# Loading the two halves of the query weights' rows from two queues in a decode attention kernel

## The chip, the cores and the metric

One core of one Trainium2 chip. The time is the device time of one execution in microseconds (us); lower is better. The kernel before takes 196.1 us (median of 5 runs, 195.98 to 196.16). In the profiles PE is the tensor engine, DVE the vector engine, ACT the scalar engine, POOL GpSimd and SP the sync engine.

## The reference

Four tokens go through a gated mix of an attention block with a sliding window and a ReGLU block. Cut to what matters:

```python
# x: [4, 1, 512], 32 query heads, 8 K/V heads, head size 128, window W = 4096
q = (x @ wq)                       # wq: [512, 4096] bf16, 4 MB: the load that the change splits
k = k_cache[:, :, Sk - W:, :]      # 4 x 8 x 4096 x 128, 32 MB
v = v_cache[:, :, Sk - W:, :]      # 32 MB
a = softmax(q k^T / sqrt(128)) v @ wo      # wo: 4 MB
b = (relu(x @ W_gate) * (x @ W_up)) @ W_down   # 3 x 1.75 MB
g = sigmoid((x * gate_w).sum(-1))
out = g * a + (1 - g) * b
```

Each input byte is used once. The sizes above, in units of 2^20 bytes, add up to 77.25, so at least 81 million bytes (81 MB) have to be moved for every execution.

## The kernel before

Everything large comes in through four SBUF slots of 128 partitions x 32 KB. All loads are issued by the sync engine, in one fixed order, on one queue (the list in which transfers wait for the DMA engines; the prediction also says ring). A load waits until the slot that it takes is free. The first four loads (query weights, K0, K1, V0) find free slots and wait for nothing.

```python
def _dma_order():
    o = [("wq",), ("x",), ("gw",), ("k", 0), ("k", 1), ("v", 0)]
    for s in range(2, NSET):
        o += [("k", s), ("v", s - 1)]
    return o + [("wg",), ("wu",), ("v", NSET - 1), ("wd",)] + ...       # wo pieces

# in _slots(): what frees a slot again
frees[n] = {"k": [("E", "KT", it[-1], 3)], "v": [("PV", it[-1])], "wq": [("Q", 1)], ...}[k]

# sync engine                                                     (cut)
elif k == "wq":
    load(("WQ",), "d_wq", slot("wq"), A_wq.rearrange("(p t) f -> p (t f)", t=4), waits=w)

# tensor engine, query matmuls                                    (cut)
def Q():
    ...
    mm(..., xT[:, 5 * q:5 * q + 4], Wq[:, q, c:c + 512], ...,
       waits=sc_free(key) + [("WQ",), ("E", "XT"), ("INIT",)] if (q, j) == (0, 0) else ())
```

In the weights' load, partition p receives four rows of `wq`, 32 KB in one piece. `x` and the gate weights `gw` are small (4 KB and 1 KB). `x` is transposed on the tensor engine, goes through a copy, a broadcast and the gate's matmuls, and then the query matmuls can run; they free the weights' slot for K2.

Of the kernel before, what the change touches and what calls it, by code (L numbers as in the profile page):

```python
# [49 lines left out]
def bc(ap, axis, n):  # L50
    shape = list(ap.shape)
    shape[axis] = n
    return ap.broadcast_to(shape)
# [105 lines left out]
# [4 lines that stand above are left out]
    return o + [("wg",), ("wu",), ("v", NSET - 1), ("wd",)] + [("wo", p) for p in range(len(WO_PIECES))]  # L163


def _slots():

    frees = [[] for _ in range(NSLOT)]
    at, wait = {}, {}
    turn = 0  # L170
    for it in _dma_order():
        k = it[0]
        if k in ("x", "gw") or (k == "wo" and it[1] > 0):
            continue
        if k == "wu":
            at[it] = at[("wg",)]
            wait[it] = wait[("wg",)]
            continue
        n = turn % NSLOT
        turn += 1  # L180
        at[it] = n
        wait[it] = list(frees[n])
        frees[n] = {"k": [("E", "KT", it[-1], 3)], "v": [("PV", it[-1])], "wq": [("Q", 1)], "wg": [("GU", 1)], "wd": [], "wo": []}[k]
    return at, wait


def _program(nc, plan, R, aps):
# [11 lines left out]
    at, slot_wait = _slots()  # L199
    order = _order()  # L200

    def slot(*it):
        return slots[:, at[it], :]
# [24 lines left out]
    def tr(key):  # L228
        return TR[trf[key] % NTR]

    def tr_free(key):
        n = trf[key] - NTR
        return [("E",) + trk[n]] if n >= 0 else []

    def scb(key):
        return SCB[scf[key] % NSC]

    def sc_free(key):
        n = scf[key] - NSC
        return [("E",) + sck[n]] if n >= 0 else [("INIT",)]  # L240

    def wo_rows(p):

        return [slice(a, b) for a, b in zip(LOW3, LOW3[1:])] if p == len(WO_PIECES) - 1 else [slice(0, 128)]

    def set_of(s):
        return s % 4, s // 4

    def ob(s):
        return banks[OB[s % 2]]  # L250

    def sync(e):
        E = _Eng(plan, e, "sp")

        def load(ev, ctr, dst, src, waits=()):
            E.op(lambda: e.dma_start(dst, src), ev=ev, waits=waits, ctr=ctr)  # L256

        for it in _dma_order():
            k = it[0]
            w = slot_wait.get(it, [])  # L260
            if k == "x":
                load(("X",), "d_x", xsb[0:4, :], A_x.rearrange("b o d -> (b o) d"))
            elif k == "gw":
                load(("GW",), "d_gw", xsb[4:5, :], gate_w.rearrange("(o p) -> o p", o=1))
            elif k == "wq":
                load(("WQ",), "d_wq", slot("wq"), A_wq.rearrange("(p t) f -> p (t f)", t=4), waits=w)
            elif k == "wg":
                load(("WG",), "d_wg", Wg, B_W_gate.rearrange("(p t) f -> p (t f)", t=4), waits=w)
            elif k == "wu":
                load(("WU",), "d_wu", Wu, B_W_up.rearrange("(p t) f -> p (t f)", t=4), waits=w)  # L270
            elif k == "wd":
                load(("WD",), "d_wd", Wd, B_W_down.rearrange("(p i) c -> p (i c)", i=14),
                     waits=w)
            elif k == "wo":
                lo, hi = WO_PIECES[it[1]]
                wo = A_wo.rearrange("(p i) c -> p (i c)", i=32)
                for n, r in enumerate(wo_rows(it[1])):
                    load(("WO", it[1], n), f"d_wo{it[1]}", Wo[r, OW * lo:OW * hi], wo[r, OW * lo:OW * hi], waits=w)
            else:
                b, qq = set_of(it[1])  # L280
                src = (A_k_cache if k == "k" else A_v_cache)[b, 4 * qq:4 * qq + 4, SK - WIN:SK, :]
                load((k.upper(), it[1]), f"d_{k}{it[1] % 3}", slot(*it), src.rearrange("h (r c) d -> r h (c d)", r=32),
                     waits=w)
        load(("OUT",), "d_out", out.rearrange("b o d -> (b o) d"), osum[:, :], waits=[("OSUM", 1), ("OSUM", 0)])
        E.wait([("OUT",)])

# [29 lines left out]
    def tensor(t):  # L316
        E = _Eng(plan, t, "pe")

        def mm(out_, lhsT, rhs, start, stop, ev=None, waits=(), pos=None):
            E.op(lambda: t.matmul(out_, lhsT, rhs, start=start, stop=stop, tile_position=pos, skip_group_check=True),  # L320
                 ev=ev, waits=waits)
# [22 lines left out]
        def Q():  # L344
            for n in range(2):
                key = ("Q", n)
                for q in range(4):
                    for j in range(4):
                        c = (4 * n + j) * 512
                        mm(banks[scb(key)][32 * j:32 * j + 4, :], xT[:, 5 * q:5 * q + 4], Wq[:, q, c:c + 512],  # L350
                           q == 0, q == 3, ev=key if (q, j) == (3, 3) else None, pos=(0, 32 * j),
                           waits=sc_free(key) + [("WQ",), ("E", "XT"), ("INIT",)] if (q, j) == (0, 0) else ())

        def QT():
            for n in range(2):
# [68 lines left out]
        def WO(p):  # L424
            lo, hi = WO_PIECES[p]
            w = [("WO", p, n) for n in range(len(wo_rows(p)))] + [("E", "OQ")]
            for x in range(lo, hi):
                i, j = x // OUTT, x % OUTT
                mm(banks[ACC][OR * j:OR * j + 4, 0:OW], oq[:, i, :], Wo[:, OW * x:OW * x + OW], False, i == 31,
                   ev=("WOP", p) if x == hi - 1 else None, waits=w if x == lo else (), pos=(0, OR * j))  # L430

        fns = dict(CONST=CONST, XT=XT, Z=Z, Q=Q, QT=QT, SC=SC, PV=PV, SW=SW, RS=RS, OQ=OQ, WO=WO, GU=GU, FFN=FFN)
        for it in order:
            if it[0] in fns:
# [41 lines left out]
    def q_dst(n, u):  # L476
        return (pe, sc)[n][:, :].rearrange("p (x u w) -> p x u w", x=8, u=4)[:, :, u, :]

    def q_src(n):
        return banks[scb(("Q", n))].rearrange("p (x w) -> p x w", x=8)  # L480
# [103 lines left out]

    def scalar(a):
        E = _Eng(plan, a, "act")

        def EQ(n):
            key = ("Q", n)
            E.op(lambda: a.activation(q_dst(n, slice(0, 4)), bc(q_src(n).unsqueeze(2), 2, 4), ACTF.Copy), ev=("QD", n),  # L590
                 waits=[key])
            plan.ev[("E", "Q", n)] = plan.ev[("QD", n)]

        def ECONST(k):
            key = ("CONST", k)
            dst = consts[k]
            E.op(lambda: a.activation(dst[:, :], banks[tr(key)][:, 0:dst.shape[1]], ACTF.Copy), ev=("E",) + key, waits=[key])

        def GWB():
            E.op(lambda: a.activation(R["gwB"][:, :, :], bc(xT[:, 4:20:5].unsqueeze(2), 2, 128), ACTF.Copy), ev=("GWB",),  # L600
                 waits=[("E", "XT")])

        def NORM(s):
            E.op(lambda: a.activation(osb[:, s, :], ob(s), ACTF.Copy), ev=("NORM", s),  # L604
                 waits=[("PV", s)])

        def GE():
            for u in range(2):
                E.op(lambda u=u: a.activation(ge[:, u, :], banks[ACC][:, 0:4], ACTF.Exp, scale=-1.0 if u == 0 else 1.0),
                     ev=("GE",) if u else None, waits=[("Z",)])  # L610

        def RELU():
            E.op(lambda: a.activation(grelu, banks[scb(("GU", 0))][:, 0:448], ACTF.Relu), ev=("RELU",),
                 waits=[("GU", 0), ("EXP", NSET - 1)])
            plan.ev[("E", "GU", 0)] = plan.ev[("RELU",)]

        def EXP(s):
            w = [("NEGMAX", s), ("E", "SC", s, 3)] + ([("E", "PT", s - 1)] if s else [("QT", 1, 1)])
            E.op(lambda: a.activation(pe[:, :], sc[:, :], ACTF.Exp, bias=negmax[:, s % 2:s % 2 + 1], scale=SCALE,  # L619
                                      accum_out=rowsum[:, s:s + 1]), ev=("EXP", s), waits=w)  # L620

        def FIN():
            E.op(lambda: a.activation(osum[:, 0:OW], banks[ACC][0:4, 0:OW], ACTF.Copy), ev=("OSUM", 0),
                 waits=[("WOP", len(WO_PIECES) - 2)])

        fns = dict(ECONST=ECONST, GWB=GWB, EQ=EQ, GE=GE, RELU=RELU, EXP=EXP, NORM=NORM, FIN=FIN)
        for it in act:
            fns[it[0]](*it[1:])

    return [("tensor", tensor), ("vector", vector), ("scalar", scalar), ("gpsimd", gpsimd), ("sync", sync)]  # L630


# [26 lines left out]
```

## Time and profile before

| | before |
|---|---|
| time, us | 196.1 |
| span of the profiled execution, us | 194.8 |
| bytes moved, MB | 81.1 |
| DMA share of the weights' stretch (6 to 11 us) | 0.97 at 419 GB/s |
| query matmuls start, us | 14.7 |
| K2 issued, us | 18.0 |

The page of the profile cuts the span into 40 slices; "DMA" is the mean busy share of the 16 DMA engines in tenths, "GB/s" what they moved. The page of the kernel before:

```profile
span 194.8 us, 1734 instructions
...
DMA  6999999999999999999999999999999999999992
GB/s 215 431 432 431 437 437 431 431 427 451 431 437 437 446 427 424 431 437 431 431 431 431 427 424 437 444 437 431 431 431 421 431 395 427 470 431 384 425 404 90
...
q1 hardware_dynamic: 3610, 81.01, 97.3%
...
slots<-in_A_wq_dram SPq DMA_DIRECT2D x1, 4096.0 KB, 12.4
```

The DMA engines are busy from the second slice to the last but one, and they move the same 430 GB/s or so throughout (384 to 470 in a slice). One queue (q1) carries everything. This kernel is a stream of transfers with compute beside it: what lengthens the stream lengthens the kernel (the table of all runs shows it: 9.6 us at 14 us are 9.9 at the end in the changed kernel, 26.2 are 26.0 in e6).

The start, from the timeline of the kernel before (start, duration, engine, line, operation; in brackets the idle time before it and what ended it):

```profile
0.80 0.40 SPq L256 DMA_DIRECT2D slots<-in_A_wq_dram  x1
1.26 0.35 SPq L256 DMA_DIRECT2D xsb<-in_A_x_dram  x1
...
13.23 0.27 PE L324 MATMUL bank<-identb,xsb 5*128 5x5 bf16 x4 [5.72 <-DMA xsb<-in_A_x_dram]
...
14.68 3.27 PE L320 MATMUL bank<-slots,xT 128*4 128x512 bf16 x32
...
18.00 0.54 SPq L256 DMA_DIRECT2D slots<-in_A_k_cache_dram  x1
```

`x`, issued second, lands only when the weights ahead of it are through; the transposes that wait for it start at 13.23 us. The query matmuls follow at 14.68 us, and K2 is issued at 18.00 us.

### The profile page before, as it was taken

What the parts mean: (1) busy time and instruction counts of PE and PEld (TensorE: products, weight loads), DVE (VectorE), ACT (ScalarE), POOL (GpSimd) and SP (SyncE); (2) the same over time, 40 slices, a digit from 0 to 9 for tenths busy, and PEclk for the clock granted to TensorE, in tenths of its full rate; (3) what the DMA queues carried; (4) which work ended last, traced back from release to release, by engine and by line L of the source; (5) the groups of instructions that cost most, each with busy time, mean ns of one, the idle gap of its engine ahead of it and who ended that gap; (6) DMA issues with size and microseconds to landing.
All of it is one profiled execution on the core that took longest, in us unless ns stands there. A gap on an engine that the chain in (4) does not pass through costs nothing.

```text
span 194.8 us, 1734 instructions
## 1 busy us (share of the span) xinstructions
PE 120.6 (62%) x723; PEld 50.6 (26%) x723; DVE 124.1 (64%) x153; ACT 27.5 (14%) x34; POOL 9.5 (5%) x25
## 2 busy tenths in 40 slices
PE   0209279474943894686468943894586466743974
PEld 0003123121411341242112411341142122311562
DVE  6103769999399809980998199819981998370010
ACT  2213000040130013001300130013001300420100
POOL 7830000000000000000000000000000000000000
PEclk9999958999999797899876999697999889997899
DMA  6999999999999999999999999999999999999992
GB/s 215 431 432 431 437 437 431 431 427 451 431 437 437 446 427 424 431 437 431 431 431 431 427 424 437 444 437 431 431 431 421 431 395 427 470 431 384 425 404 90
DMA packets 3616, 81.10 MB, mean 416 GB/s; under 512 B 401, under 2 KB 666, under 8 KB 794
## 3 DMA queue, kind: packets, MB, share of 16 engines
q1 hardware_dynamic: 3610, 81.01, 97.3%
q8 instruction: 5, 0.08, 0.2%
q14 instruction: 1, 0.01, 0.0%
HBM read 81.01 MB, written 0.00 MB: 416 GB/s over the span
## 4 chain that ended last, share of the span: by engine, by line
DMA 54%; DVE 31%; PE 9%; issue 4%; SPq 0%; ACT 0%
DMA slots<-in_A_k_cache_dram 38%; DVE kt L491 21%; DMA slots<-in_A_wo_dram 10%; PE bank L320 7%; DMA xsb<-in_A_x_dram 6%; DVE sc L527 5%; DVE qblk L517 1%; PE bank L324 1%; DVE pT L542 1%; DVE rd L531 1%; SPq L256 0%; DVE negmax L537 0%; ACT gwB L600 0%; DVE osum L577 0%; DVE mx L527 0%
## 5 line engine op out<-in xcount | busy, mean ns | idle before, releaser
L491 DVE STREAM_TRANSPOSE kt<-slots 128x2048 f32<-128x2048 f32 x32 | 73.7, 2305 | 28.1 <-DMA slots<-in_A_k_cache_dram 28.0
L320 PE MATMUL bank<-kt,qblk 128*128 128x512 bf16 x256 | 72.1, 434 | 27.9 <-DVE kt L491 27.9
L320 PEld LDWEIGHTS bank<-kt,qblk 128*128 128x128 bf16 x256 | 25.2, 107 | 69.7 <-DVE kt L491 36.0
L320 PE MATMUL bank<-slots,pT 128*64 128x512 bf16 x256 | 32.3, 410 | 5.7 <-DMA slots<-in_A_v_cache_dram 5.7
L619 ACT ACTIVATE pe<-sc,negmax 128x2048 bf16<-128x2048 bf16 x8 | 16.0, 2002 | 60.1 <-DVE negmax L537 60.1
L527 DVE CUSTOM_DVE_ANT_0 sc<-bank,maskf 128x512 bf16<-128x512 f32 x32 | 21.0, 658 | 3.8 <-PE bank L320 3.7
L320 PEld LDWEIGHTS bank<-slots,pT 128*64 128x64 bf16 x256 | 15.1, 118 | 23.2 <-issue 13.4
L542 DVE STREAM_TRANSPOSE pT<-pe 128x2048 bf16<-128x2048 bf16 x8 | 18.5, 2312 | 2.2 <-ACT pe L619 2.2
L604 ACT ACTIVATE osb<-bank 128x512 bf16<-128x512 f32 x8 | 4.8, 597 | 81.5 <-PE bank L320 81.5
L320 PE MATMUL bank<-rd,grpb 128*128 128x32 bf16 x8 | 1.6, 194 | 22.1 <-DVE rd L531 22.1
L555 DVE TENSOR_TENSOR oq<-bank,recip 64x128 bf16<-64x128 f32 x2 | 0.9, 434 | 12.3 <-PE bank L320 12.2
L320 PEld LDWEIGHTS bank<-rd,grpb 128*128 128x128 bf16 x8 | 0.8, 98 | 25.7 <-DVE rd L531 25.7
L495 DVE COPY xT<-bank 128x20 bf16<-128x20 bf16 x1 | 0.2, 171 | 8.0 <-PE bank L324 8.0
L320 PE MATMUL bank<-slots,oq 128*4 128x256 bf16 x64 | 4.0, 272 | 2.0 <-DMA slots<-in_A_wo_dram 2.0
L320 PE MATMUL bank<-slots,xT 128*4 128x512 bf16 (+1 forms) x64 | 5.0, 467 | 0.0
L320 PE MATMUL bank<-maskr,maskl 128*128 128x512 bf16 x1 | 0.6, 609 | 5.9 <-POOL maskr L296 5.9
L517 DVE TENSOR_SCALAR qblk<-bank 32x64 uint32<-32x64 uint32 x16 | 2.9, 215 | 2.1 <-PE bank L324 2.1
L324 PE MATMUL bank<-identb,xsb 5*128 5x5 bf16 x4 | 0.3, 168 | 5.7 <-DMA xsb<-in_A_x_dram 5.7
L577 DVE CAST osum<-bank 4x256 bf16<-4x256 f32 x1 | 0.4, 418 | 5.2 <-PE bank L320 5.2
L320 PEld LDWEIGHTS bank<-slots,oq 128*4 128x4 bf16 x64 | 2.5, 84 | 3.5 <-DMA slots<-in_A_wo_dram 2.9
L296 POOL TENSOR_SCALAR_AFFINE_SELECT fold<-fold 128x256 bf16<-128x256 bf16 x8 | 3.3, 417 | 1.1
L486 DVE MEMSET qblk<- 128x2304 uint32 x1 | 2.0, 1978 | 1.3 <-PEq L644 1.3
(59 smaller groups left out, 40.3 us busy)
## 6 DMA issues: line engine op xcount, KB each, us to landing
slots<-in_A_k_cache_dram SPq DMA_DIRECT2D x8, 4096.0 KB, 25.1
slots<-in_A_v_cache_dram SPq DMA_DIRECT2D x8, 4096.0 KB, 30.5
slots<-in_A_wq_dram SPq DMA_DIRECT2D x1, 4096.0 KB, 12.4
slots<-in_A_wo_dram SPq DMA_DIRECT2D x1, 2176.0 KB, 17.1
slots<-in_B_W_gate_dram SPq DMA_DIRECT2D x1, 1792.0 KB, 19.7
slots<-in_B_W_up_dram SPq DMA_DIRECT2D x1, 1792.0 KB, 23.6
slots<-in_B_W_down_dram SPq DMA_DIRECT2D x1, 1792.0 KB, 18.5
slots<-in_A_wo_dram SPq DMA_DIRECT2D x1, 1152.0 KB, 19.5
```

What stands on the lines that cost most here:

```text
L296: op(lambda: e.affine_select(dst, src, pattern, cmp, fill, base=base, channel_multiplier=mult), ev)
L320: E.op(lambda: t.matmul(out_, lhsT, rhs, start=start, stop=stop, tile_position=pos, skip_group_check=True), ev=ev, waits=waits)
L324: E.op(lambda: t.transpose(out_, in_, idn), ev=ev, waits=waits)
L486: E.op(lambda: v.memset(qblk[:, :, :, :, :].rearrange("p s h c e -> p (s h c e)"), 0.0), ev=("QZ",))
L491: E.op(lambda: v.transpose(kt[:, f, :].bitcast(FP32), slot("k", s)[:, 4096 * f:4096 * f + 4096].bitcast(FP32)), ev=("E", "KT", s, f), waits=w)
L517: E.op(lambda dst=dst, r=r, g=g: v.tensor_scalar(dst, src[r, g, 0:B, :, :], 0, None, op0=ALU.bitwise_or), ev=("E",) + keys[1] if (q, g) == ...
L527: E.op(lambda: v.tensor_tensor_reduce(sc[:, 512 * f:512 * f + 512], banks[scb(key)], R["maskf"][:, :], 1.0, -3.0e38, ALU.add, ALU.max, mx4 ...
L531: E.op(lambda: v.tensor_tensor(rd32[:, :, :], bc(R["own8"][:, :].unsqueeze(2), 2, 4), bc(mx4[:, :].unsqueeze(1), 1, 8), ALU.mult), ev=("MA ...
L542: E.op(lambda: v.transpose(pT[:, s % 2, :], pe[:, :]), ev=("E", "PT", s), waits=[("EXP", s)] + ([("PV", s - 2)] if s >= 2 else []))
L555: E.op(lambda g=g, r=r: v.tensor_tensor(oq[r, :, :].rearrange("p i b -> p b i"), banks[tr(key)][0:64, 128 * g:128 * g + 128].rearrange("p ...
L604: E.op(lambda: a.activation(osb[:, s, :], ob(s), ACTF.Copy), ev=("NORM", s), waits=[("PV", s)])
L619: E.op(lambda: a.activation(pe[:, :], sc[:, :], ACTF.Exp, bias=negmax[:, s % 2:s % 2 + 1], scale=SCALE, accum_out=rowsum[:, s:s + 1]), ev= ...
```

## The change

The intent is to have two queues bring in the first 4 MB: partitions 0 to 63 from the sync queue, 64 to 127 from the scalar queue, as its first instruction, so that neither sequencer has to issue the whole load.

```diff
+    wq_all = A_wq.rearrange("(p t) f -> p (t f)", t=4)
 ...
             elif k == "wq":
-                load(("WQ",), "d_wq", slot("wq"), A_wq.rearrange("(p t) f -> p (t f)", t=4), waits=w)
+                load(("WQ", 0), "d_wq", slot("wq")[0:64, :], wq_all[0:64, :], waits=w)
 ...
-     waits=sc_free(key) + [("WQ",), ("E", "XT"), ("INIT",)] if (q, j) == (0, 0) else ())
+     waits=sc_free(key) + [("WQ", 0), ("WQ", 1), ("E", "XT"), ("INIT",)] if (q, j) == (0, 0) else ())
 ...
     def scalar(a):
         E = _Eng(plan, a, "act")
+        E.op(lambda: a.dma_start(slot("wq")[64:128, :], wq_all[64:128, :]), ev=("WQ", 1), waits=..., ctr="d_wq1")
```

More of the change, by code (lines that the diff above doesn't have):

```diff
@@ L586, in scalar @@
         E = _Eng(plan, a, "act")
+        E.op(lambda: a.dma_start(slot("wq")[64:128, :], wq_all[64:128, :]), ev=("WQ", 1), waits=slot_wait.get(("wq",), []), ctr="d_wq1")
         def EQ(n):
```

## The prediction

> **What bounds the kernel now.** The DMA engines, nearly from end to end. The page's 40 slices show DMA 9 in every slice but the first and the last, at 421 to 451 GB/s in most; the queue table gives 81.01 MB on one queue, 97.3% of 16 engines' span. In the trace's DMA records 16 packets are in flight at every moment from 2.2 to 190.4 us. A 32 KB packet takes 1.213 us on its engine, so 16 engines move 432 GB/s and 81.01 MB cost 187.4 us; the rest of the 194.8 us span is the start (the first query-weight packet starts at 1.81 us and takes about 2 us) and the tail (last landing at 192.2, then matmuls, copy and output). DVE (64%) and PE (62%) have slack: before most K tiles DVE idles for a landing (28.0 us in all, groups by line).
>
> **The front.** The sync queue issues the query weights at 0.80 us, x at 1.26, the gate weights at 1.66, then K0, K1, V0. The weights and x both land at about 13.1 us, because x stands behind them in the same ring (x's four landing events are at 12.9 to 13.1). Then: transposes, copy, broadcast, gate matmuls, 1.5 us together; the query matmuls start at 14.68. They release the slot for K2, issued at 18.0 us. But K0, K1 and V0, 12 MB or 29 us of transfer, are still queued then, so the queue would stay fed if Q ended some 20 us later.
>
> **What the change does.** No byte is removed. The sync queue keeps 2 MB and the scalar queue gets 2 MB, issued at about 0.8 us too, before ACT's table load (ACT is next needed at 6.57 us: hidden, even if 0.4 us are added). [...] Issue is 0.40 us here, once, so at most 0.1 to 0.3 us can be won at the start. x will stand behind half of the weights in its ring; with the rings taking turns it lands up to one packet (1.2 us) earlier, so Q may start 0 to 1.4 us earlier. That is off the critical path: it doesn't advance the saturated stream.
>
> **The danger.** Each half covers 64 partitions. [...] If all 16 engines work on the same half at once, the 4 MB could run below 432 GB/s. At half rate they would take about 19 us in place of 9.7, and since the stream is the bound, nearly all of that would reach the end (about 205 us). [...] No trace here shows a 64-partition load; I give it about one chance in five to cost over 2%.
>
> **Prediction.** 196.1 us; 8 in 10 between 195.2 and 200.5. Faster by over 2%: 0.02; within 2%: 0.80; slower: 0.18.
>
> **What would show it.** Right: the queue table has a second queue with 2.1 MB; wq's halves land at 12.5 to 14 us; x lands at 11.5 to 13.2; DMA share 9 from the second slice on; slice rates in the first 15 us unchanged; the end moves under 0.7 us; DVE's waits for K from K2 on merely keep their sum within 2 us. Wrong: 32 KB packets of the weights longer than 1.3 us, GB/s under 400 in slices 2 and 3, and the whole schedule after shifted by that loss. [...]

The forecast's sum came to 196.1 us, no change: the same bytes at the measured rate, and at most 0.1 to 0.3 us won at the start, an estimate from the 0.40 us that the issue took. The half rate (19 us is about twice the 9.7 us) and the "one chance in five" stand as estimates. That the rings take turns was an assumption then; the packet records of the changed kernel show it in rounds 1 to 6 (table below).

## More of the kernel before

Busy times in stretches of the kernel before (us, then busy time and count by engine, clock, DMA share, GB/s; a packet is counted whole, so a figure of one stretch can be some per cent off):

```profile
6.00:11.00 5.00, 1.03 (x3) 0.22 (x3) 0.00 (x0) 1.04 (x3) 3.87 (x10) 1.00 0.97 419
11.00:16.00 5.00, 1.76 (x24) 0.86 (x28) 0.17 (x1) 0.87 (x3) 0.83 (x2) 1.00 1.01 434
```

## The result, and the profile after

The changed kernel takes 205.97 us (median of 5 runs, 205.83 to 206.08) against 196.1 us (5 runs): a ratio of 1.0505, 95% interval 1.049 to 1.0519. It is 5% slower, and the prediction's range (195.2 to 200.5) does not hold the result. Ratios here are the mean time of one kernel's fast runs over that of the other's fast runs of the same rounds, so they are not quite the ratio of the medians that are quoted. Executions over 1.5% slower than the fastest of the same kernel are left out of the means.

The page after:

```profile
span 204.8 us, 1736 instructions
...
DMA  8999899999999999999999999999999999999992
GB/s 198 211 205 205 321 480 429 410 410 445 454 429 410 416 456 448 413 416 429 461 435 410 422 432 454 422 422 416 467 429 416 419 422 414 469 422 407 425 402 88
...
q1 hardware_dynamic: 3546, 78.92, 92.6%
q10 hardware_dynamic: 80, 2.10, 4.6%
...
slots<-in_A_wq_dram SPq DMA_DIRECT2D x1, 2048.0 KB, 22.3
slots<-in_A_wq_dram ACTq DMA_DIRECT2D x1, 2048.0 KB, 19.6
```

The two rows of slices have to be read together. The DMA share is 8 or 9 from the first slice on, as if nothing had happened; but in slices 2 to 4 these busy engines move 205 to 211 GB/s, where they moved 431 before. From the sixth slice on the rate is the old one. The bytes are the same (78.92 + 2.10 = 81.02 MB).

The stretches after:

```profile
6.00:11.00 5.00, 1.03 (x3) 0.23 (x3) 0.00 (x0) 1.04 (x3) 3.87 (x10) 1.00 0.95 210
11.00:16.00 5.00, 0.00 (x0) 0.00 (x0) 0.00 (x0) 0.00 (x0) 0.83 (x2) 1.00 0.98 216
16.00:21.00 5.00, 0.00 (x0) 0.00 (x0) 0.00 (x0) 0.00 (x0) 0.00 (x0) 1.00 1.02 216
```

Nearly the same DMA share (0.95 against 0.97), half the bytes (210 against 419 GB/s). The timeline after shows both queues issuing at once, and a start that is 10 us late:

```profile
0.80 0.59 SPq L258 DMA_DIRECT2D slots<-in_A_wq_dram  x1
0.80 0.54 ACTq L589 DMA_DIRECT2D slots<-in_A_wq_dram  x1
...
23.11 0.26 PE L326 MATMUL bank<-identb,xsb 5*128 5x5 bf16 x4 [15.60 <-DMA xsb<-in_gate_w_dram]
...
24.57 3.58 PE L322 MATMUL bank<-slots,xT 128*4 128x512 bf16 x32
...
28.19 0.54 SPq L258 DMA_DIRECT2D slots<-in_A_k_cache_dram  x1
```

Issuing half of the rows was not cheaper either: 0.59 us on sync and 0.54 us on scalar, against 0.40 us for the whole, and the sync engine came to `x` at 1.44 us in place of 1.26. (The number of rows is not all that sets this: K2, with all 128 partitions, takes 0.54 us in both kernels.)

The trace also records each DMA packet (start, duration, size, queue). The weights are 128 packets of 32 KB. Ordered by start they fall into eight rounds of 16, as many as the page counts engines; so I take a round as one packet for each engine, though the records do not name a packet's engine. My count from these records (median duration in us, queue of all 16 packets):

```
            before                        after
round   starts us     took   queue   starts us     took   queue
  0     1.81-2.77     1.99   sync    2.12-3.09     2.14   scalar
  1     3.75-4.33     1.23   sync    3.92-5.12     2.56   scalar
  2     4.97-5.56     1.21   sync    6.46-7.63     2.37   sync
  3     6.18-6.76     1.21   sync    8.82-9.99     2.37   scalar
  4     7.39-7.97     1.21   sync    11.19-12.36   2.37   sync
  5     8.60-9.18     1.21   sync    13.56-14.72   2.37   scalar
  6     9.81-10.39    1.21   sync    15.92-17.09   2.38   sync
  7     11.02-11.60   1.21   sync    18.30-19.51   2.55   sync
last packet ends      12.82                        22.11
```

Two things stand in this table. A packet takes twice its time. And all 16 packets of a round come from the same queue: from round 1 to 6 the queues take turns packet by packet, and all engines take the same turn. They are in step to within half a packet (starts within 1.2 us, packets of 2.37 us). So for half of the time from round 2 to 6 all 16 engines write partitions of one half; in the other half of the time one round is ending while the next begins, and packets of both halves are in flight. Sixteen packets of 32 KB in 2.37 us are 221 GB/s; in 1.213 us they are 432 GB/s.

### The profile page after: what moved, and what is told of

It reads as the page before. It is cut to its first block, busy times and chain, and to the rows that moved or that the text cites. A ratio compares the mean times of both kernels' runs of the same rounds, so it can differ in the third digit from the quotient of the medians.

```text
span 204.8 us, 1736 instructions
## 1 busy us (share of the span) xinstructions
PE 124.4 (61%) x723; PEld 51.9 (25%) x723; DVE 124.7 (61%) x153; ACT 27.5 (13%) x34; POOL 9.5 (5%) x25
## 3 DMA queue, kind: packets, MB, share of 16 engines
q1 hardware_dynamic: 3546, 78.92, 92.6%
## 4 chain that ended last, share of the span: by engine, by line
DMA 49%; DVE 24%; PE 20%; issue 5%; SPq 1%; ACT 0%
DMA slots<-in_A_k_cache_dram 24%; PE bank L322 18%; DVE kt L493 17%; DMA slots<-in_A_v_cache_dram 14%; DMA xsb<-in_gate_w_dram 10%; DVE sc L529 4%; PE bank L326 2%; DVE qblk L519 1%; SPq L258 1%; DVE oq L557 0%; DVE rd L533 0%; DVE negmax L539 0%; ACT gwB L603 0%; DVE osum L579 0%; DVE mx L529 0%
## 5 line engine op out<-in xcount | busy, mean ns | idle before, releaser
L493 DVE STREAM_TRANSPOSE kt<-slots 128x2048 f32<-128x2048 f32 x32 | 73.7, 2305 | 22.0 <-DMA slots<-in_A_k_cache_dram 21.9
L322 PEld LDWEIGHTS bank<-kt,qblk 128*128 128x128 bf16 x256 | 24.7, 106 | 74.5 <-DVE kt L493 41.5
L322 PE MATMUL bank<-slots,pT 128*64 128x512 bf16 x256 | 35.2, 437 | 5.7 <-DMA slots<-in_A_v_cache_dram 5.7
L322 PEld LDWEIGHTS bank<-slots,pT 128*64 128x64 bf16 x256 | 16.1, 126 | 26.3 <-issue 17.7
```

Source lines behind the costliest of these rows:

```text
L322: E.op(lambda: t.matmul(out_, lhsT, rhs, start=start, stop=stop, tile_position=pos, skip_group_check=True), ev=ev, waits=waits)
L493: E.op(lambda: v.transpose(kt[:, f, :].bitcast(FP32), slot("k", s)[:, 4096 * f:4096 * f + 4096].bitcast(FP32)), ev=("E", "KT", s, f), waits=w)
```

## The experiments

The theories that the texts below name:

- P (partitions): the rate is set by which partitions are being written at one moment; "in lockstep" in the texts below means that all engines are in the same round.
- Q (queues): two queues on one engine, taking turns, cost the rate.
- L (late start): the query matmuls start late, and that is what reaches the end.
- S (source): the memory side is slow for these rows.

Edits are given against the changed kernel if nothing else is said. "K0 delay" in the table at the end is measured in the packet records. e5 to e8 and e10 to e12 are two runs each, and the times of e10, e11 and e12 unclear; what is read from these three rests on their packet records.

### e1_one_queue: both halves on the sync queue

```diff
-  (scalar) a.dma_start(slot("wq")[64:128, :], wq_all[64:128, :])
+  (sync)   load(("WQ", 1), "d_wq1", slot("wq")[64:128, :], wq_all[64:128, :], waits=w)    # after the first half
```

> Both 64-partition halves on the sync queue, one after the other; nothing on the scalar queue. Theory P (16 engines write 64 partitions, [...] so the weights move at half rate): 205.9 us, weight packets about 2.37 us as in the changed kernel, about 215 GB/s until 21 to 22 us. Theory Q (two queues on one engine cost the rate, by taking turns): 196.1 us, packets 1.21 us. Theory L (only the late start of the query matmuls costs time): it has no packet slowdown to explain and expects 196.

Measured: 206.8 us, ratio 1.0541 (1.0526 to 1.0555). The stretches of this run:

```profile
6.00:11.00 5.00, 1.03 (x3) 0.22 (x3) 0.00 (x0) 1.04 (x3) 3.88 (x10) 1.00 1.02 210
11.00:16.00 5.00, 0.00 (x0) 0.00 (x0) 0.00 (x0) 0.00 (x0) 0.83 (x2) 1.00 0.99 210
```

The second queue is gone and the rate is still half. Theory Q falls. It is 0.8 us slower than the changed kernel: six of the eight rounds took 2.55 or 2.56 us a packet here, two there. The records show which: a round that follows one of the same half takes 2.55 or 2.56 us (rounds 1 and 7 of the changed kernel, all but the first and round 4 here), a round that follows one of the other half takes 2.37 or 2.38 us (rounds 2 to 6 there, only round 4 here). Four rounds by 0.19 us are nearly all of the 0.8 us. So the handovers, in which both halves are in flight, gain a little; why they gain no more is not shown.

### e2_columns: two queues, split by columns

```diff
-  slot("wq")[0:64, :],   wq_all[0:64, :]        # sync
-  slot("wq")[64:128, :], wq_all[64:128, :]      # scalar
+  slot("wq")[:, 0:8192],     wq_all[:, 0:8192]
+  slot("wq")[:, 8192:16384], wq_all[:, 8192:16384]
```

> Two queues, but split by columns: each half is all 128 partitions by 16 KB. Theory P: full rate, 196.0 to 196.4 us, 16 KB packets about 0.61 us, query matmuls start within 1.5 us of the kernel before. Theory Q: about 205 us, packets of double time.

Measured: 196.35 us, ratio 1.0007 (0.9994 to 1.0019). The page of this run:

```profile
DMA  6999999999999999999999999999999999998992
GB/s 215 430 431 430 430 430 437 457 420 450 443 430 437 432 437 433 430 437 430 430 430 430 427 430 430 437 430 430 430 430 427 430 389 423 478 430 375 441 394 71
```

Two queues taking turns move 430 GB/s in the second slice; the 16 KB packets took 0.61 us. With all 128 partitions in each half, two queues cost nothing, and they gain nothing.

### e3_window: partitions 32 to 95 first

```diff
-  sync [0:64], scalar [64:128]
+  sync [32:96], then sync [0:32], then sync [96:128]
```

> One sync queue: partitions 32 to 95 first (64 partitions[...]), then 0 to 31, then 96 to 127. Theory P: the first 2 MB run at full rate (packets 1.21 us), the other 2 MB at half rate (2.37 us), so half of the loss: 201.0 us (200.5 to 201.6). A theory that any 64-partition load is slow (too few rows for each engine): 205.9 us. Theory Q: 196.1.

Measured: 201.47 us, ratio 1.0272 (1.0258 to 1.0286): half of the loss. In the packet records the four rounds of the window are through at 8.02 us (7.98 in the kernel before), then, after one round in between (2.03 us), packets take 2.36 to 2.56 us. So a 64-partition load isn't slow in itself; it depends on which 64.

### e4_late_x: the late start by itself

The edit is against the kernel before, and slows no load:

```diff
-    o = [("wq",), ("x",), ("gw",), ("k", 0), ("k", 1), ("v", 0)]
+    o = [("wq",), ("k", 0), ("x",), ("gw",), ("k", 1), ("v", 0)]
```

> The kernel before, but x and the gate weights are issued behind K0 in the same ring, so that x lands near 23 us as in the changed kernel, with no load slowed. Theory P: the end does not move, 196.1 us within 0.7, though the query matmuls start near 24.5 us in place of 14.7 and K2 is issued about 10 us later. Theory L: about 205 us.

Measured: 197.09 us, ratio 1.0048 (1.0033 to 1.0063). From the timeline and the page of this run:

```profile
24.32 3.58 PE L320 MATMUL bank<-slots,xT 128*4 128x512 bf16 x32
```

```profile
GB/s 214 435 442 442 436 435 449 449 442 428 418 428 335 428 435 423 428 425 428 428 428 428 428 449 432 435 449 449 428 442 428 425 374 434 472 428 390 426 399 74
```

The query matmuls start at 24.32 us, as late as in the changed kernel, but the end moves by 0.9 us and not by 9.9. So L explains at most a tenth. I had expected under 0.7. About half of the 0.9 us is seen in the 13th slice (335 GB/s): K3 is issued only at 59.70 us here, and in the packet records fewer than 14 packets are in flight from 60.7 to 61.7 us, which costs about 0.5 us of the engines' time; the other 0.4 us is not traced. As query matmuls 9.6 us later just let the queue run dry, I estimate the queue's reserve at a little under 10 us, not the 20 us that the prediction gave it. In the changed kernel the stream is late as well, and no such gap shows.

### e5_quarters and e6_eighths: fewer neighbouring partitions for each load

```diff
-  sync [0:64], scalar [64:128]
+  sync [0:32], [32:64], [64:96], [96:128]             # e5_quarters
+  sync [0:16], [16:32], ..., [112:128]                # e6_eighths
```

> Sync queue only, the weights as four loads of 32 partitions. Theory P [...]: again half rate, 206 to 208 us, no worse than the two halves. A theory that the rate follows the number of partitions of a load (64 gave half, so 32 give a quarter): about 29 us lost, 225 us.

Measured: 206.34 us, ratio 1.0524 (1.0487 to 1.0561). Quarters cost what halves cost (205.97 us in the changed kernel, 206.8 in e1), and moved 210 GB/s from 6 to 11 us, as these did.

> Sync queue only, the weights as eight loads of 16 partitions, one packet for each engine[...]. Theory P with engines in lockstep: quarter rate, packets about 4.8 us, some 29 us lost, 225 us (215 to 230[...]). A theory that splitting as such halves the rate: 206.

Measured: 222.08 us, ratio 1.1327 (1.1275 to 1.1379). Its stretches:

```profile
6.00:11.00 5.00, 1.05 (x3) 0.24 (x3) 0.00 (x0) 1.04 (x3) 3.91 (x10) 1.00 0.93 105
11.00:16.00 5.00, 0.00 (x0) 0.00 (x0) 0.00 (x0) 0.00 (x0) 0.83 (x2) 1.00 0.93 105
```

DMA share 0.93, a quarter of the rate (105 against 419 GB/s). A packet takes 4.6 us (16 of 32 KB in that time are 114 GB/s), all 16 engines still in step (starts within 1 us). A rule of "each split halves the rate" falls (quarters are no slower than halves), and so does "the rate follows the number of partitions" (64 and 32 give the same, 210 GB/s). Why 16 neighbours take twice as long as 32 is not shown.

### e7_even_odd and e12_even_odd_one_queue: even and odd partitions

```diff
-  slot("wq")[0:64, :],   wq_all[0:64, :]        # sync
-  slot("wq")[64:128, :], wq_all[64:128, :]      # scalar
+  slot("wq")[0:128:2, :], wq_all[0:128:2, :]    # sync
+  slot("wq")[1:128:2, :], wq_all[1:128:2, :]    # scalar (e12: sync, after the first)
```

> Two queues, each 64 partitions, but the even and the odd ones[...]. Theory P with lockstep: half rate, 204 to 207 us. Theory P [...]: full rate, 196.2 us.

The two forms of P differ in whether all partitions of a load count or those written at one moment.

Measured: 196.43 us, ratio 1.0019 (0.999 to 1.0048). Packets take 1.22 us in the third round and 1.21 us from the fourth on, and the stretch from 6 to 11 us reads as that of the kernel before:

```profile
6.00:11.00 5.00, 1.05 (x3) 0.24 (x3) 0.00 (x0) 1.04 (x3) 3.91 (x10) 1.00 0.97 419
```

> Even partitions, then odd ones, both on the sync queue: does the full rate of the even and odd halves depend on two queues? If the partitions alone decide: 196.2 to 196.8 us, packets 1.21 us. If it was the taking turns of two queues [...]: about 206 us.

Measured: 196.4 us, ratio 1.0012 (0.9993 to 1.0031). So halves of 64 partitions are free, on one queue as on two, when they are the even and the odd ones (419 GB/s from 6 to 11 us in both runs, as in the kernel before; packets of 1.21 us in e12). The lockstep form of P, as I had written it for e7, is refuted: it expected half rate. It rested on an assumption of how the rows are dealt to the engines, which no run shows. After the first round the engines do go in step to within half a packet (starts within 0.6 us in e7), but the records do not name the engine, so which of a load's partitions are written together here stays open.

### e8_window_src: the same source rows, another destination

Its output is wrong, which doesn't matter for the time. Edit against e3_window:

```diff
-  [32:96] <- rows of 32:96,  [0:32] <- rows of 0:32
+  [32:96] <- rows of 0:64,   [0:32] <- rows of 64:96
```

> Wrong result on purpose: destinations as in the window experiment (32 to 95, then 0 to 31, then 96 to 127), but the first load reads the source rows 0 to 63, which the slow first half of the changed kernel read. Theory P (destination partitions decide): 201.5 us, as the window experiment, first 2 MB with packets of 1.21 us. Theory S (the memory side decides: these 64 source rows in a row are slow to read): packets of about 2.4 us for the first load too, 206 us.

Measured: 201.5 us, ratio 1.0277 (1.0247 to 1.0307), as e3_window. The source rows that the changed kernel reads slowly are read at full rate when they go to partitions 32 to 95 (median packets of 1.21 to 1.23 us after the first round). Its page shows it in the second slice, where the changed kernel moved 211 GB/s:

```profile
GB/s 209 367 236 237 452 458 452 419 419 416 419 419 445 460 439 422 425 419 419 425 425 452 452 435 425 419 419 425 425 445 448 439 390 421 459 425 406 436 399 99
```

Theory S falls for the halves; in the loads of 16 partitions (e6, e10, e11) source and destination changed together, and there it rests on this run. (Its output passed the comparison all the same, presumably because these small random inputs leave the attention nearly uniform, which was not tested; it is not a valid kernel.)

### e9_early_x: does the front chain matter the other way?

Edit against the kernel before: the weights whole on sync; `x` and `gw` move to the scalar queue as its first two instructions.

```diff
+  (scalar) a.dma_start(xsb[0:4, :], A_x...);  a.dma_start(xsb[4:5, :], gate_w...)
```

> The weights whole on the sync queue, and x and the gate weights from the scalar queue as its first instructions, so that they land near 3 us and the query matmuls start when the weights land (about 13.2 in place of 14.7 us). Theory P (the stream of transfers sets the end): 196.1 us within 0.4. If the front chain were on the critical path: about 194.7.

Measured: 196.12 us, ratio 0.9998 (0.9984 to 1.0012). From its timeline:

```profile
13.21 3.58 PE L320 MATMUL bank<-slots,xT 128*4 128x512 bf16 x32 [3.77 <-DMA slots<-in_A_wq_dram]
```

The query matmuls start 1.5 us earlier than in the kernel before, and the end doesn't move.

### e10_stride4 and e11_stride8: 16 partitions, so that it is certain which are written together

```diff
-  sync [0:64], scalar [64:128]
+  sync [32:96:4], [33:96:4], [34:96:4], [35:96:4], then [0:32], [96:128]     # e10_stride4
+  sync [0:128:8], [1:128:8], ..., [7:128:8]                                   # e11_stride8
```

> Sync queue only. The window 32 to 95 as four loads of 16 partitions with a step of 4 (one packet for each engine[...]), then 0 to 31 and 96 to 127 as before. Theory P: the first 2 MB at full rate, 201.3 to 202 us, as the window experiment, where eight loads of 16 neighbouring partitions ran at a quarter. A theory that loads of 16 partitions are slow as such: the window takes about 19 us, over 215 us in all.

Measured: 202.93 us, ratio 1.0345 (1.0325 to 1.0365). Loads of 16 partitions aren't slow as such: the second took 1.22 us a packet (the first round is longer in the kernel before too, 1.99 us against 1.21), against 4.6 us for 16 neighbours in e6. But it missed what I expected by about 1 us. In the third and fourth load some packets took up to 2.2 us, and the window was through at 9.04 us instead of 8.02. I have no explanation for that.

> Sync queue only, eight loads of 16 partitions with a step of 8 (0, 8, ..., 120 and so on), one packet for each engine, so that it is certain which partitions are written together. [...] half rate, about 206 us. [...] 196 to 197 us.

Two answers: half rate (about 206 us) and full rate (196 to 197 us).

Measured: 206.53 us, ratio 1.0529 (1.0509 to 1.0548). Sixteen packets are in flight and, after the first round, take 2.36 to 2.55 us. Its stretch from 6 to 11 us:

```profile
6.00:11.00 5.00, 1.03 (x3) 0.23 (x3) 0.00 (x0) 1.04 (x3) 3.88 (x10) 1.00 1.03 210
```

A load is 16 packets here, as many as are in flight, so but for the handovers from load to load 0, 8, ..., 120 (then 1, 9, ..., 121 and so on) are written together, and the rate is half: 210 GB/s, where the even and the odd partitions moved 419. So that a load spreads from partition 0 to 120 is not enough for the full rate. Why a step of 8 is slow and a step of 2 is not, is not shown.

### All runs in one table

"K0 delay" is how much later than in the kernel before the first round of K0's packets ends (14.03 us there), which is when the weights are out of the way. The second column gives the partitions of each load of the weights, "neighbours" being partitions in a row.

| run | partitions of a load | K0 delay, us | change of the median, us |
|---|---|---|---|
| changed kernel | 64 neighbours | 9.6 | +9.9 |
| e1_one_queue | 64 neighbours | 10.2 | +10.7 |
| e5_quarters | 32 neighbours | 10.0 | +10.3 |
| e11_stride8 | 16 with a step of 8 | 10.2 | +10.3 |
| e6_eighths | 16 neighbours | 26.2 | +26.0 |
| e3_window | 32 to 95; then twice 32 neighbours | 5.2 | +5.3 |
| e8_window_src | 32 to 95; then twice 32 neighbours | 5.2 | +5.4 |
| e10_stride4 | 32 to 95 as four of 16 with a step of 4; then twice 32 neighbours | 6.5 | +6.7 |
| e2_columns | all 128, half of the columns | -0.1 | +0.2 |
| e7_even_odd | 64 with a step of 2 | 0.2 | +0.4 |
| e12_even_odd_one_queue | 64 with a step of 2 | 0.2 | +0.2 |
| e9_early_x | all 128 | 0.0 | -0.1 |
| e4_late_x | all 128 | 0.1 | +0.9 |

In every run but e4_late_x (its gap comes later) the delay of the stream at 14 us is the delay at the end, within half a microsecond. No split beat the kernel before: e2, e12 and e7, the nearest, lie 0.07 to 0.19% above it, which is within the noise. As the stream of 81 MB is what bounds it, none was to be expected.

## Why the prediction was wrong

- **What bounds the kernel: right.** The stream of transfers sets the end. The table shows it: a delay of the stream goes through to the end nearly whole, while the query matmuls 1.5 us earlier (e9) changed nothing and 9.6 us later (e4) cost 0.9 us.
- **"At most 0.1 to 0.3 us can be won at the start": right in that nothing was to be won, wrong in its sign.** The first packet starts at 2.12 us in place of 1.81, and the two issues took 0.59 and 0.54 us in place of 0.40.
- **The step that failed: the time of the weights' transfer.** The central figure costed the 4 MB at 432 GB/s, 9.7 us, and listed "slice rates in the first 15 us unchanged" among the signs of being right. They measured 205 to 221 GB/s: the last packet ended at 22.11 us in place of 12.82, which is 9.3 of the 9.9 us. The remaining 0.6 us: K0's first round adds 0.3, and the rest isn't traced.
- **The danger was in the text, with its size, and was given the wrong weight.** "At half rate they would take about 19 us in place of 9.7 [...] (about 205 us)" is what happened, at 205.97. But it got "about one chance in five", on an argument about engines out of step or interleaving finely. The runs showed no fine interleaving: whole 32 KB packets alternate, and all 16 engines take the same half in the same round. They are out of step by up to 1.2 us, half of a packet's 2.37 us, and nearly everything was lost all the same: a round after the other half took 2.37 or 2.38 us, one after the same half 2.55, where full rate is 1.21. What in the kernel before would have hinted at the common rounds: its own packet rounds, whose starts lie within 0.6 us round after round, from the second to the last of the table above. I had looked at these packets for their duration and not for their order.
- **x "lands up to one packet (1.2 us) earlier": wrong, it landed about 10 us later** (transposes at 23.11 in place of 13.23 us), with the half that it stands behind.
- **"The queue would stay fed if Q ended some 20 us later": too generous.** By e4 the reserve is an estimated 10 us or a little less.
- **"DVE's waits for K from K2 on merely keep their sum within 2 us": wrong.** It fell from 28.0 to 21.9 us (groups by line). That wait is on an engine that isn't the bottleneck, and it says nothing of the time.

What is shown is that the destination partitions of a load decide the rate, and that queues (e1 206.8 us, e2 196.35), source rows (e8 201.5 us, e3 201.47) and the late start (e4 197.09 us) don't. In e6 and e11, where a load has one packet for each engine (4.6 us, and 2.36 to 2.55 us), the partitions of a load are those in flight together; for the larger loads it is not shown which of them are. Why the destination decides is not shown by any run: the full rate (1.21 us a packet), the half (2.36 to 2.56) and the quarter (4.6) are what was measured for each set; two loads of e10's window, with packets of up to 2.2 us, fit none of these. A pair of loads that keep one half of the engines on 0 to 63 while the other half is on 64 to 127 was not built.

## What to carry to other kernels

Before splitting a load by partitions, ask which partitions each part takes: here two halves ran at full rate when they were split by columns (430 GB/s in the second slice, e2) or into even and odd partitions (419 from 6 to 11 us, e7 and e12), and at half when each was 64 neighbours, on two queues as on one (210, changed kernel and e1). Split by columns, or with a step of 2, if a split is wanted at all; it gained nothing here, where the engines were already saturated (DMA share 0.97 at 419 GB/s). And read the DMA share only beside the GB/s: an engine whose packets take twice their time counts as busy all the same (share 0.95 at 210 GB/s).
